# Another map of on-chip memory for one decode step with its gradients: V of seven groups resident, K in two slots

## The chip, the cores and the metric

The kernel runs on one core of a Trainium2 chip. The time is the device time of one execution in microseconds (us); less is better. The core has TensorE (PE in the profile) for matrix products, VectorE (DVE), ScalarE (ACT), GpSimd (POOL) and SyncE (SP), and 16 DMA engines that move data between DRAM and on-chip memory. Two queues feed those DMA engines here: q1, filled by SP, and q0, filled by POOL.

## The reference

One token `x` of 448 numbers goes through a layer norm, attention over a cache (16 query heads, 8 groups of keys and values, head size 256, the last 4096 of 32768 positions), a residual sum, a second layer norm and a gated feed-forward layer without a nonlinearity. Cut to what matters:

```
q = (layernorm(x) @ wq), 16 heads of 256
scores = q . k[:, :, Sk-W:, :] / 16 ;  p = softmax(scores) ;  o = p . v[:, :, Sk-W:, :]
h = x + o @ wo
y = h + ((n @ w_gate) * (n @ w_up)) @ w_down,   n = layernorm(h)
outputs: y, and the gradients of x, k_cache, v_cache, wq, wo, w_gate, w_up, w_down for a given grad_out
```

All data is bf16. The outputs `out_2` and `out_3` are the gradients of the two caches (called dK and dV here) in the caches' full shape, 134 MB each: zero outside the window of 4096 positions, computed inside it. So 235 MB of the outputs are zeros that must be written to DRAM all the same.

## The kernel before

The zeros go out on SP's queue (`FILL`). One memset on VectorE makes a tile `zeros`; then 18 transfers (`fill`, line 63) copy it into the gradients of the caches, 16 KB to a packet, at most eight in flight at a time. A rest of one region is cut over different sets of partitions, which spreads it unevenly over the DMA engines, and two pieces of it (`fill_rest`) go on POOL's queue. Everything else that moves, loads and computed outputs, is issued by POOL (`IO`), in the order in which POOL's program stands; an issue waits there until its source is written or its destination is free, and those behind it wait too.

On chip, the large data lives in nine slots of 16 KB per partition (`S`), an array `Mt` and a ring `Rt`. A slot holds K or V of one group: 128 partitions, 32 positions each, 256 numbers per position. The tables say which group uses which slot:

```
K_SLOT = [6, 7, 8, 6, 7, 8, 6, 7]
V_SLOT = [0, 1, 2, 3, 4, 5, 8, 8]
```

The work has three parts.

The first part runs over the eight groups. `scores` transposes K through TensorE in eight steps of four positions (`products`, line 294: a bank of transposes, an evacuation by ScalarE or VectorE in turn, products with q). `softmax` follows, and then `moments` (lines 346 to 361): in 16 steps of two positions VectorE scales K by the probabilities, and TensorE sums products of V with the scaled K and with the probabilities. The loop issues `softmax(g)`, `scores(g + 1)`, `moments(g)`, with K loaded two groups ahead and V one ahead. V of groups 6 and 7 both pass through slot 8, in halves (`load_V_halves`).

The turn comes next: the output projection with `wo`, the second layer norm, the gate and up products, and the way back through them to the gradient of the attention output and of q. `wo`, `w_gate` and `w_up` are loaded into K slots and into the ring when the last moments are done with them. `spread` makes rows out of columns and copies them to all partitions.

The second part again runs over the groups. It transposes V (line 607) and multiplies it with the gradient of the output (line 612), forms 32 products of rows (line 636), two positions to a PSUM tile of two banks, and evacuates dV and dK apart, ScalarE the one and VectorE the other (line 239 and 241, the helper `evac`). dV is staged in the slot of this group's V, dK in slot 6 or 7, and both are issued to DRAM (line 641). V of groups 6 and 7, which no longer stand on chip, are loaded again after groups 1 and 2 (`load_V`, line 643). Between the groups stand the outer products that make the gradients of the weights (`side`, `outer`, lines 516 and 517), through two staging buffers, and the parts that need `wq` and `w_down` a second time (`dxn_load`, `dxn_part`, `ffn_out`).

Of the kernel before, what the change touches and what calls it, by code (L numbers as in the profile page):

```python
# [13 lines left out]
D = 448  # L14
NI = 7
# [11 lines left out]
NS = 9  # L27
NV = 6
# [6 lines left out]
K_SLOT = [6, 7, 8, 6, 7, 8, 6, 7]  # L35
V_SLOT = [0, 1, 2, 3, 4, 5, 8, 8]
# [3 lines left out]
def kernel(  # L40
# [8 lines left out]
    small = ctx.enter_context(tc.tile_pool(name="small", bufs=2))  # L49
    ps = ctx.enter_context(tc.tile_pool(name="ps", bufs=1, space=bass.MemoryType.PSUM))  # L50

    x_bf = const.tile([1, D], bf16, tag="rowa", name="x_bf")
    FILL.dma_start(out=x_bf[:], in_=A_x.rearrange("a b d -> (a b) d"))
    go_bf = const.tile([1, D], bf16, tag="rowb", name="go_bf")
    FILL.dma_start(out=go_bf[:], in_=grad_out.rearrange("a b d -> (a b) d"))
# [25 lines left out]
    S = const.tile([128, NS, SLOT], bf16)  # L81
    Mt = const.tile([128, G, 2, 2 * Dh], bf16)
    Rt = const.tile([128, SLOT], bf16)

    def slot(k):
        return S[:, k, :]

    def slot_kv(k):
        return S[:, k, :].rearrange("p (t d) -> p t d", d=Dh)

# [12 lines left out]
    def load_V_halves(g):  # L103
        for h in range(2):
            t = slice(h * T // 2, (h + 1) * T // 2)
            IO.dma_start(out=Vw[g][:, t, :], in_=A_v_cache[0, g, Sk - W:, :].rearrange("(p t) d -> p t d", t=T)[:, t, :])
# [5 lines left out]
    wq_sb = S[:, 4:6, :].rearrange("p a b -> p (a b)")[:, 0:NI * HQ]  # L112
# [4 lines left out]
    wd0 = S[:, 3, 0:FC * D].rearrange("p (c n) -> p c n", n=D)  # L117
    wd_rows = B_w_down.rearrange("(s j m) n -> j s (m n)", s=2, j=128)
    IO.dma_start(out=wd0.rearrange("p (s m) n -> p s (m n)", s=2), in_=wd_rows)

# [5 lines left out]
    ones_bf = const.tile([128, 128], bf16)  # L126
# [46 lines left out]
    def rows_to_half(row, xe):  # L173
        t = ps.tile([128, NI], f32, tag="tmp", bufs=1)
        for i in range(NI):
            c = xe[i // 4][:, (i % 4) * 128:(i % 4 + 1) * 128]
            V_.tensor_copy(out=c.rearrange("o (m r) -> o m r", r=2), in_=half_cols(row, i))
            P_.matmul(t[:, i:i + 1], lhsT=c, rhs=ones_f[0:1, 0:1], start=True, stop=True)
        return t
# [64 lines left out]
    xe0 = [Mt[0:1, G - 2 + k].rearrange("p f c -> p (f c)").bitcast(f32) for k in range(2)]  # L244
    xX = const.tile([128, NI], f32)
    V_.tensor_copy(out=xX[:], in_=rows_to_half(x_bf[:], xe0)[:])
    gX = const.tile([128, NI], f32)
    V_.tensor_copy(out=gX[:], in_=rows_to_half(go_bf[:], xe0)[:])
# [17 lines left out]
    q_rows = const.tile([H, Dh], bf16)  # L266
    do_rows = const.tile([H, Dh], bf16)


# [7 lines left out]

    def kt_buf():
        k = kt_ctr[0] % NB
        kt_ctr[0] += 1  # L280
        return Rt[:, k * 1024:(k + 1) * 1024].rearrange("p (i h c) -> p i h c", i=4, h=2)

    def pk_buf():
        k = NB + pk_ctr[0] % NB
        pk_ctr[0] += 1
        return Rt[:, k * 1024:(k + 1) * 1024].rearrange("p (i h d) -> p i h d", i=2, h=2)

    def products(Xw, vecT, g, out_ps):

        for q in range(8):  # L290
            tr = ps.tile([128, 4, 2, 128], bf16, tag="tr", bufs=2)
            for i in range(4):
                for dh in range(2):
                    P_.transpose(tr[:, i, dh, :], Xw[:, 4 * q + i, dh * 128:(dh + 1) * 128], ident_bf[:])  # L294
            xt = kt_buf()
            evac(xt, tr[:])
            for i in range(4):
                for dh in range(2):
                    P_.matmul(out_ps[:, 4 * q + i, :], lhsT=xt[:, i, dh, :], rhs=vecT[:, 4 * g + dh:4 * g + dh + 3:2],
                              start=(dh == 0), stop=(dh == 1))  # L300
# [6 lines left out]
    def scores(g):  # L307
        sT[g] = fps.tile([128, T, 2], f32, tag="sT", bufs=2, name="sT")
        products(Kw[g], qT, g, sT[g])

    def softmax(g):
# [19 lines left out]
        pf = small.tile([128, T, 2], f32, tag="p_f")  # L331
# [344 lines left out]
```

## Time and profile before

| | |
|---|---|
| median of 3 runs | 800.72 us (800.29 to 801.64) |
| the profiled execution: its time, and its span | 800.97 us, 799.2 us |
| bytes moved by the DMA engines | 336.46 MB, mean 421 GB/s |
| read from and written to DRAM | 55.18 MB, 280.59 MB |
| PE, PEld, DVE, ACT, POOL busy | 466.5, 269.7, 378.0, 170.0, 37.6 us |
| first part's last K and V issue by POOL | 251.00 us |
| first and last dV or dK issue | 473.31 and 700.14 us |

The page cuts the span into 40 slices of 20 us: a digit is the busy share in tenths, `DMA` the mean of the 16 engines, `GB/s` what they moved. Its part 3 gives each queue's packets, bytes and the time of those packets as a share of 16 engines' span. A window's line gives start and end, length, busy time of PE, PEld, DVE, ACT and POOL with their instructions in brackets, the granted clock of TensorE, the DMA share and GB/s. A timeline's line gives the start, the duration, engine, line and instruction, and in square brackets how long the engine was idle before and what ended that. An issue's line gives its count, the size of one, and the median us from issue to landing.

### The profile page before, as it was taken

The numbers are of one execution on the slowest core, as the hardware profiler recorded it, in microseconds if no ns is written. First come the engines' busy times: TensorE is split into PE (matmuls) and PEld (weight loads), VectorE is DVE, ScalarE is ACT, GpSimd is POOL, SyncE is SP. The second block draws the span as 40 slices with busy tenths as digits, with TensorE's granted clock in tenths as the row PEclk, the third lists the DMA queues.
The fourth block names the chain that finished last, engine by engine and source line by source line (L and its number), as shares of the span: only waits on it lengthen the run. The fifth ranks groups of instructions, "written<-read, shape, count | busy, mean of one in ns | idle before, by whom it ended". The sixth has DMA issues, their size and how long they took to land.

```text
span 799.2 us, 10787 instructions
## 1 busy us (share of the span) xinstructions
PE 466.5 (58%) x4384; PEld 269.7 (34%) x4419; DVE 378.0 (47%) x1150; ACT 170.0 (21%) x261; POOL 37.6 (5%) x78
## 2 busy tenths in 40 slices
PE   3659767999997644532788645489963625500000
PEld 3545535655664322332576212135510101100000
DVE  5129554778866411668423568375463623500000
ACT  0220202211220000300432322245532413300000
POOL 3000000000000010000001000001000000000000
PEclk9999696999998875555556555555555555555555
DMA  8999999999999999999999999999999999999996
GB/s 340 430 425 430 427 430 430 429 425 429 428 424 421 429 423 429 430 424 431 428 425 423 411 427 432 421 431 420 428 429 426 429 429 417 427 425 429 428 430 294
DMA packets 23815, 336.46 MB, mean 421 GB/s; under 512 B 1501, under 2 KB 1503, under 8 KB 3559
## 3 DMA queue, kind: packets, MB, share of 16 engines
q1 hardware_dynamic: 14550, 231.98, 68.4%
q0 software_dynamic: 9216, 103.80, 30.9%
q8 instruction: 34, 0.56, 0.2%
q14 instruction: 15, 0.12, 0.0%
HBM read 55.18 MB, written 280.59 MB: 420 GB/s over the span
## 4 chain that ended last, share of the span: by engine, by line
DMA 17%; issue 16%; PE 11%; DVE 8%; ACT 3%; POOL 1%; POOLq 0%; ACTq 0%; DVEq 0%
DMA out_dram<-S 7%; DMA Rt<-in_A_wq_dram 4%; DMA S<-in_A_wo_dram 3%; DMA S<-in_A_v_cache_dram 3%; ACT S L239 3%; PE tr L607 3%; PE d_ps L636 2%; DVE S L473 2%; DVE S L241 2%; PE dp L612 1%; PE MT L350 1%; DVE Rt L461 1%; DVE Rt L552 1%; PE dh_ps L188 1%; PE ao L421 1%
## 5 line engine op out<-in xcount | busy, mean ns | idle before, releaser
L636 PE MATMUL d_ps<-R,S 32*128 32x512 bf16 x256 | 121.8, 611 | 88.9 <-DVE S L241 87.7
L350 PE MATMUL MT<-Rt,S 128*128 128x512 bf16 x477 | 137.4, 393 | 7.7 <-DMA S<-in_A_v_cache_dram 7.2
L346 DVE TENSOR_SCALAR Rt<-S,pf 128x256 bf16<-128x256 bf16 x512 | 117.3, 282 | 20.3 <-PE MT L350 12.1
L241 DVE CAST S<-d_ps 128x512 bf16<-128x512 f32 x128 | 86.4, 688 | 54.0 <-ACT S L239 38.8
L239 ACT CAST S<-d_ps 128x512 bf16<-128x512 f32 x128 | 75.0, 586 | 149.3 <-PE d_ps L636 149.1
L636 PEld LDWEIGHTS <-S 32*128 32x128 bf16 x256 | 26.0, 116 | 155.5 <-issue 153.8
L607 PE MATMUL tr<-ident_bf,S 128*128 128x128 bf16 x512 | 66.3, 305 | 17.8 <-ACT S L239 17.8
L294 PE MATMUL tr<-ident_bf,S 128*128 128x128 bf16 x512 | 51.7, 260 | 38.8 <-DMA S<-in_A_k_cache_dram 36.6
L353 PEld LDWEIGHTS <-S 128*128 128x128 bf16 x512 | 47.5, 98 | 57.8 <-issue 3.9
L607 PEld LDWEIGHTS <-S 128*128 128x128 bf16 x512 | 48.5, 137 | 31.9 <-issue 31.9
L294 PEld LDWEIGHTS <-S 128*128 128x128 bf16 x512 | 40.3, 118 | 40.1 <-DMA S<-in_A_k_cache_dram 37.1
L353 PE MATMUL acc<-pT_all,S 128*128 128x2 bf16 x512 | 47.3, 165 | 4.9 <-DMA S<-in_A_v_cache_dram 2.8
L239 ACT COPY Rt<-tr 128x1024 bf16<-128x1024 bf16 x32 | 32.4, 1012 | 71.8 <-PE tr L294 71.4
L356 PE MATMUL acc<-pT_all,S 128*128 128x2 bf16 x512 | 46.9, 164 | 0.0
L239 ACT COPY S<-tr 128x1024 bf16<-128x1024 bf16 x32 | 32.4, 1013 | 49.2 <-PE tr L607 32.2
L241 DVE COPY Rt<-tr 128x1024 bf16<-128x1024 bf16 x32 | 22.0, 688 | 39.5 <-PE tr L294 35.2
L350 PEld LDWEIGHTS <-S 128*128 128x128 bf16 x512 | 35.1, 99 | 15.7 <-DMA S<-in_A_v_cache_dram 7.2
L241 DVE COPY S<-tr 128x1024 bf16<-128x1024 bf16 x32 | 22.0, 688 | 37.1 <-PE tr L607 37.0
L358 ACT CAST Mt<-MT 128x512 bf16<-128x512 f32 x8 | 4.7, 586 | 149.0 <-PE MT L350 132.9
L356 PEld LDWEIGHTS <-S 128*128 128x128 bf16 x512 | 30.8, 97 | 0.2
L612 PEld LDWEIGHTS <-S 128*128 128x128 bf16 x512 | 20.7, 108 | 23.2 <-ACT S L239 16.9
L612 PE MATMUL dp<-doT,S 128*128 128x2 bf16 x512 | 23.7, 169 | 6.1 <-ACT S L239 5.2
(200 smaller groups left out, 394.9 us busy)
## 6 DMA issues: line engine op xcount, KB each, us to landing
out_dram<-zeros SPq DMA_DIRECT2D x15, 14336.0 KB, 164.8
out_dram<-S POOLq DMA_DIRECT2D x16, 2048.0 KB, 29.4
S<-in_A_k_cache_dram POOLq DMA_DIRECT2D x8, 2048.0 KB, 28.4
S<-in_A_v_cache_dram POOLq DMA_DIRECT2D x8, 2048.0 KB, 60.1
out_dram<-zeros SPq DMA_DIRECT2D x1, 10240.0 KB, 95.2
S<-in_A_v_cache_dram POOLq DMA_DIRECT2D x4, 1024.0 KB, 14.2
S<-in_A_wq_dram POOLq DMA_DIRECT2D x1, 3584.0 KB, 15.2
S<-in_A_wo_dram POOLq DMA_DIRECT2D x2, 1792.0 KB, 20.7
```

The costliest lines, as they stand in the source:

```text
L188: P_.matmul(d3[:, :, (7 * s + i) // 2], lhsT=lt, rhs=ident_f[:, s::2], start=(first and n == 0), stop=(n == 2 * NI - 1), skip_group_check= ...
L239: S_.copy(out=out, in_=in_)
L241: V_.tensor_copy(out=out, in_=in_)
L294: P_.transpose(tr[:, i, dh, :], Xw[:, 4 * q + i, dh * 128:(dh + 1) * 128], ident_bf[:])
L346: V_.tensor_scalar(out=pk[:, i, h, :], in0=K[:, t, :], scalar1=pf[:, t, h:h + 1], scalar2=None, op0=ALU.mult)
L350: P_.matmul(MT[:, hf, :], lhsT=Vv[:, t, hf * 128:(hf + 1) * 128], rhs=pk[:, i, :, :].rearrange("p h d -> p (h d)"), start=(t == 0), stop=( ...
L353: P_.matmul(acc[:, 2 * hf:2 * hf + 2], lhsT=Vv[:, t, hf * 128:(hf + 1) * 128], rhs=pT_all[:, g, t, :], start=(t == 0 and hf == 0), stop=(t ...
L356: P_.matmul(acc[:, 4 + dk:7 + dk:2], lhsT=K[:, t, dk * 128:(dk + 1) * 128], rhs=pT_all[:, g, t, :], start=False, stop=(t == T - 1), skip_g ...
L473: V_.tensor_tensor_reduce(out=wo_b(b), in0=wo_b(b), in1=dh_bc[:], scale=1.0, scalar=0.0, op0=ALU.mult, op1=ALU.add, accum_out=doW[:, b:b + 1])
L607: P_.transpose(tr[:, i, dh, :], Vw[g][:, 4 * q + i, dh * 128:(dh + 1) * 128], ident_bf[:])
L612: P_.matmul(dp[:, 4 * q + i, :], lhsT=xt[:, i, dh, :], rhs=doT[:, 4 * g + dh:4 * g + dh + 3:2], start=(dh == 0), stop=(dh == 1))
L636: P_.matmul(d_ps[:, i, :, :].rearrange("p w d -> p (w d)"), lhsT=rows[32 * k:32 * k + 32, a, :], rhs=R[32 * k:32 * k + 32, :], start=True, ...
```

## The change

On-chip memory becomes one array `BIG`: nine slots and a tail. V of groups 0 to 6 has slots 0 to 6 from first load to last use; slots 7 and 8 are for K, each loaded in two halves (`load_halves`) after the moments of the group two before, and V of group 7 takes slot 7 after the moments of group 6 and is the one V that is loaded a second time, into slot 2. The ring of six buffers lies at the end of the tail, `w_gate` and `w_up` behind `wo` in slot 8 and the tail.

In the first part, `moments(g)` issues the eight steps of `scores(g + 1)` after its own steps 4 to 11, each with `issue_after` behind the last matmul of its step, and `softmax(g + 1)` with step 11. `wo` comes in four transfers. At the turn, `spread` keeps its result in PSUM, where the reductions of the weights read it, and is done for one weight after the other. In the second part one position has one PSUM bank with dV and dK, which one engine evacuates, four banks in turn; dV and dK are staged side by side in slots 7 and 8 for even groups and 0 and 1 for odd ones. The outer products have one spare buffer and the slots that come free, and are spread over the groups in another way; their issues and the second loads of `w_down` and `wq` stand behind the dV and dK of their group. Small rows move into the tail, and some small tiles have one buffer where they had two.

```diff
-NS = 9
-NV = 6
...
-K_SLOT = [6, 7, 8, 6, 7, 8, 6, 7]
-V_SLOT = [0, 1, 2, 3, 4, 5, 8, 8]
+KS = 7
+TAIL = 9 * SLOT
+SIZE = TAIL + 10624
+K_SLOT = [KS + g % 2 for g in range(G)]
+V_SLOT = [0, 1, 2, 3, 4, 5, 6, KS]
...
+    BIG = const.tile([128, SIZE], bf16)
+    x_bf = BIG[0:1, TAIL + 2048:TAIL + 2048 + D]
+    FILL.dma_start(out=x_bf, in_=A_x.rearrange("a b d -> (a b) d"))
+    go_bf = BIG[0:1, TAIL + 3072:TAIL + 3072 + D]
+    FILL.dma_start(out=go_bf, in_=grad_out.rearrange("a b d -> (a b) d"))
...
-    def load_V_halves(g):
+    def load_halves(dst, cache, g):
         for h in range(2):
             t = slice(h * T // 2, (h + 1) * T // 2)
-            IO.dma_start(out=Vw[g][:, t, :], in_=A_v_cache[0, g, Sk - W:, :].rearrange("(p t) d -> p t d", t=T)[:, t, :])
+            IO.dma_start(out=dst[:, t, :], in_=cache[0, g, Sk - W:, :].rearrange("(p t) d -> p t d", t=T)[:, t, :])
...
-    wq_sb = S[:, 4:6, :].rearrange("p a b -> p (a b)")[:, 0:NI * HQ]
+    wq_sb = BIG[:, 4 * SLOT:4 * SLOT + NI * HQ]
     IO.dma_start(out=wq_sb, in_=flat_rows(A_wq))
     load_K(0)
     load_V(0)
     load_K(1)
-    wd0 = S[:, 3, 0:FC * D].rearrange("p (c n) -> p c n", n=D)
+    load_V(1)
+    wd0 = slot(6)[:, 0:FC * D].rearrange("p (c n) -> p c n", n=D)
     wd_rows = B_w_down.rearrange("(s j m) n -> j s (m n)", s=2, j=128)
     IO.dma_start(out=wd0.rearrange("p (s m) n -> p s (m n)", s=2), in_=wd_rows)
+    load_V(2)
...
+    def products(Xw, vecT, g, out_ps, q):
+        tr = ps.tile([128, 4, 2, 128], bf16, tag="tr", bufs=2)
+        for i in range(4):
+            for dh in range(2):
+                P_.transpose(tr[:, i, dh, :], Xw[:, 4 * q + i, dh * 128:(dh + 1) * 128], ident_bf[:])
...
+    def scores(g, q):
+        if q == 0:
+            sT[g] = fps.tile([128, T, 2], f32, tag="sT", bufs=2, name="sT")
+        products(Kw[g], qT, g, sT[g], q)
...
-                    P_.matmul(acc[:, 4 + dk:7 + dk:2], lhsT=K[:, t, dk * 128:(dk + 1) * 128], rhs=pT_all[:, g, t, :],
+                    mm = P_.matmul(acc[:, 4 + dk:7 + dk:2], lhsT=K[:, t, dk * 128:(dk + 1) * 128], rhs=pT_all[:, g, t, :],
                               start=False, stop=(t == T - 1), skip_group_check=True)
+            if g + 1 < G and 4 <= c < 12:
+                with tc.issue_after(mm.ins):
+                    scores(g + 1, c - 4)
+                if c == 11:
+                    softmax(g + 1)
...
-    woA = S[:, 6, 0:16 * D].rearrange("p (b n) -> p b n", n=D)
-    woB = S[:, 8, 0:16 * D].rearrange("p (b n) -> p b n", n=D)
-    wg_sb = S[:, 7, 0:NI * HF]
-    wu_sb = Rt[:, 0:NI * HF]
-    bc2 = [S[:, 7, NI * HF:NI * HF + F].rearrange("p (i c) -> p i c", i=2), Rt[:, NI * HF:NI * HF + F].rearrange("p (i c) -> p i c", i=2)]
+    A0 = KS * SLOT
+    WB = [0, 9, 18, 27, 32]
 
     def wo_b(b):
-        return woA[:, b, :] if b < 16 else woB[:, b - 16, :]
-
-    scores(0)
-    rows16(qT, q_rows[:], SCALE)
+        o = A0 + b * D if b < 18 else A0 + SLOT + (b - 18) * D
+        return BIG[:, o:o + D]
+
+    def load_wo(k):
+        o = A0 + (k // 2) * SLOT + (k % 2) * 9 * D
+        n = WB[k + 1] - WB[k]
+        IO.dma_start(out=BIG[:, o:o + n * D].rearrange("p (b n) -> p b n", n=D), in_=wo_v[:, WB[k]:WB[k + 1], :])
+
+    G0 = A0 + SLOT + 14 * D
+    wg_sb = BIG[:, G0:G0 + NI * HF]
+    wu_sb = BIG[:, G0 + NI * HF:G0 + 2 * NI * HF]
+    bc2 = [BIG[:, TAIL + w * F:TAIL + (w + 1) * F].rearrange("p (i c) -> p i c", i=2) for w in range(2)]
+
+    for q in range(8):
+        scores(0, q)
+    softmax(0)
     for g in range(G):
-        if g + 1 < NV:
-            load_V(g + 1)
+        if g + 3 < G - 1:
+            load_V(g + 3)
+        moments(g)
         if g + 2 < G:
-            load_K(g + 2)
-        if g >= NV:
-            load_V_halves(g)
-        if g == G - 1:
-            IO.dma_start(out=woA, in_=wo_v[:, 0:16, :])
-        softmax(g)
-        if g + 1 < G:
-            scores(g + 1)
-        moments(g)
+            load_halves(Kw[g + 2], A_k_cache, g + 2)
+        if g + 2 == G:
+            load_halves(Vw[G - 1], A_v_cache, G - 1)
...
-    IO.dma_start(out=woB, in_=wo_v[:, 16:32, :])
+    for k in (0, 2, 1, 3):
+        load_wo(k)
...
-    def spread(dst, src, nb, rows2, row_blocks):
-
-        for b0 in range(0, nb, 4):
-            n = min(4, nb - b0)
-            t = fps.tile([2, 4, 128], f32, tag="sT", bufs=2, name="t")
+    def spread(src, nb, b0):
+
+        bc = tps.tile([128, 2, 1024], f32, tag="bc", name="bc")
+        for b1 in range(b0, min(b0 + 8, nb), 4):
+            n = min(4, nb - b1)
+            t = tps.tile([2, 4, 128], f32, tag="t", name="t")
             for j in range(n):
-                P_.matmul(t[:, j, :], lhsT=src[:, b0 + j:b0 + j + nb + 1:nb], rhs=ident_bf[:], start=True, stop=True)
-            evac(row_blocks[:, b0:b0 + n, :], t[:, 0:n, :])
-        for i2 in range(2):
-            for b0 in range(0, nb, 4):
-                n = min(4, nb - b0) * 128
-                t = fps.tile([128, 512], f32, tag="sT", bufs=2, name="t")
-                P_.matmul(t[:, 0:n], lhsT=Par[:, i2, :], rhs=rows2[:, b0 * 128:b0 * 128 + n], start=True, stop=True)
-                evac(dst[:, i2, b0 * 128:b0 * 128 + n], t[:, 0:n])
-
-    rows2 = [S[0:2, k, 16 * D:16 * D + HF] for k in (6, 8)]
-    for w in range(2):
-        spread(bc2[w], dgu[:, w, :], NI, rows2[w], rows2[w].rearrange("s (j m) -> s m j", m=NI))
+                P_.matmul(t[:, j, :], lhsT=src[:, b1 + j:b1 + j + nb + 1:nb], rhs=ident_bf[:], start=True, stop=True)
+            r = small.tile([2, 4, 128], bf16, tag="R", name="r")
+            evac(r[:, 0:n, :], t[:, 0:n, :])
+            for i2 in range(2):
+                P_.matmul(bc[:, i2, (b1 - b0) * 128:(b1 - b0 + n) * 128], lhsT=Par[:, i2, :], rhs=r[:, 0:n, :].rearrange("p b c -> p (b c)"),
+                          start=True, stop=True)
+        return bc
...
+        bc = spread(dgu[:, w, :], NI, 0)
+        wv = w_sb.rearrange("p (i j m) -> p i m j", i=NI, m=NI)
         for i in range(NI):
-            V_.tensor_tensor_reduce(out=wv[:, i, :], in0=wv[:, i, :], in1=bc2[w][:, i % 2, :], scale=1.0, scalar=0.0,
+            V_.tensor_tensor_reduce(out=wv[:, i], in0=wv[:, i], in1=bc[:, i % 2, 0:HF].rearrange("p (m j) -> p m j", m=NI), scale=1.0, scalar=0.0,
                                     op0=ALU.mult, op1=ALU.add, accum_out=P2[:, w, i:i + 1])
+        for i2 in range(2):
+            S_.copy(out=bc2[w][:, i2, :].rearrange("p (j m) -> p m j", m=NI), in_=bc[:, i2, 0:HF].rearrange("p (m j) -> p m j", m=NI))
...
+    wd1 = slot(3)[:, 0:FC * D].rearrange("p (c n) -> p c n", n=D)
+
+    def wd_load():
+        IO.dma_start(out=wd1.rearrange("p (s m) n -> p s (m n)", s=2), in_=wd_rows)
...
+    PAIR = [KS, 0, KS, 0, KS, 0, KS, 0]
     side = {
-        0: [o67_job(0, 0, 4), o67_job(0, 4, 7), lambda: dxn_part(0, 4), lambda: dxn_load(4, 7)],
-        1: [lambda: dxn_part(4, 7), dx_out],
-        2: [o5_job(0), o5_job(8)],
-        3: [o5_job(16), o5_job(24)],
-        4: [lambda b=b: outer(o8[b // 7], b, b + 7, lambda n: dh2_bc[:], hh, D) for b in (0, 7)],
-        5: [o4_job(0), o4_job(2)],
-        6: [o4_job(4), o4_job(6)],
+        0: [o67_job(spare, 1, 4, 7)],
+        1: [o67_job(spare, 0, 0, 4)],
+        2: [o67_job(spare, 0, 4, 7), lambda: load_V(G - 1)],
+        3: [o5_job(spare, 0), wd_load],
+        4: [lambda: dxn_load(0, 4), ffn_out, o5_job(spare, 8), o5_job(half(3, 0), 16), o5_job(half(3, 1), 24)],
+        5: [lambda: dxn_load(4, 7), lambda: dxn_part(0, 4), o8_job(spare, 0), o8_job(half(4, 0), 7), o4_job(half(4, 1), 0)],
+        6: [lambda: dxn_part(4, 7), dx_out, o4_job(half(5, 0), 2), o4_job(half(5, 1), 4), o4_job(spare, 6)],
         7: [],
     }
-    ffn_out()
-    o67_job(1, 0, 4)()
-    o67_job(1, 4, 7)()
-    dxn_load(0, 4)
+    o67_job(spare, 1, 0, 4)()
...
-        R = small.tile([128, 2 * Dh], bf16, tag="R")
-        S_.copy(out=R[:], in_=R_ps[:])
-        stg = [Vw[g], slot_kv(6 + g % 2)]
-        for c in range(T // 2):
-            d_ps = bps.tile([128, 2, 2, Dh], f32, tag="d2", bufs=2)
-            for i in range(2):
-                t = 2 * c + i
-                k, a = t // 8, t % 8
-                P_.matmul(d_ps[:, i, :, :].rearrange("p w d -> p (w d)"), lhsT=rows[32 * k:32 * k + 32, a, :], rhs=R[32 * k:32 * k + 32, :],
-                          start=True, stop=True)
-            for w in range(2):
-                evac(stg[w][:, 2 * c:2 * c + 2, :], d_ps[:, :, w, :])
+            P_.matmul(R_ps[:, k * Dh:(k + 1) * Dh], lhsT=ex[:].rearrange("h a r -> h (a r)"), rhs=rr, start=True, stop=True)
+        R = Rb[:, g % 2, :]
+        S_.copy(out=R, in_=R_ps[:])
+        pair = BIG[:, PAIR[g] * SLOT:(PAIR[g] + 2) * SLOT].rearrange("p (w t d) -> p w t d", w=2, d=Dh)
+        for t in range(T):
+            d_ps = bps.tile([128, 2, Dh], f32, tag="d2", bufs=4)
+            k, a = t // 8, t % 8
+            P_.matmul(d_ps[:].rearrange("p w d -> p (w d)"), lhsT=rows[32 * k:32 * k + 32, a, :], rhs=R[32 * k:32 * k + 32, :],
+                      start=True, stop=True)
+            evac(pair[:, :, t, :], d_ps[:])
         for w, o in ((0, out_3), (1, out_2)):
-            IO.dma_start(out=o[0, g, Sk - W:, :].rearrange("(p t) d -> p t d", t=T), in_=stg[w])
-        if 1 <= g <= G - NV:
-            load_V(NV + g - 1)
...
```

## The prediction

> **What bounds the kernel now.** I read four views in this order. First the page's slices and its part on the queues, to see whether an engine or the transfers fill the span:
>
> ```profile
> PEclk9999696999998875555556555555555555555555
> DMA  8999999999999999999999999999999999999996
> GB/s 340 430 425 430 427 430 430 429 425 429 428 424 421 429 423 429 430 424 431 428 425 423 411 427 432 421 431 420 428 429 426 429 429 417 427 425 429 428 430 294
> ...
> q1 hardware_dynamic: 14550, 231.98, 68.4%
> q0 software_dynamic: 9216, 103.80, 30.9%
> ...
> HBM read 55.18 MB, written 280.59 MB: 420 GB/s over the span
> ```
>
> Between the first slice and the last the 16 DMA engines are full, at 411 to 432 GB/s, whatever TensorE's granted clock does. The two queues' packets took 68.4 + 30.9 = 99.3% of the 16 engines' span. The bound is the sum of all transfers; what is left to ask is whether anything lies behind them. So, second, a table of windows, with the end in stretches of its own:
>
> ```profile
> 216.00:252.00 36.00, 34.31 (x437) 21.96 (x442) 25.93 (x107) 5.87 (x10) 2.65 (x5) 0.95 1.00 424
> 500.00:700.00 200.00, 127.45 (x638) 46.42 (x636) 96.79 (x174) 73.88 (x118) 12.22 (x23) 0.50 1.01 426
> 700.00:739.00 39.00, 0.00 (x0) 0.00 (x0) 0.00 (x0) 0.00 (x0) 0.53 (x1) 0.50 1.01 425
> 739.00:782.00 43.00, 0.00 (x0) 0.00 (x0) 0.00 (x0) 0.00 (x0) 0.00 (x0) 0.50 1.01 428
> 782.00:799.20 17.20, 0.00 (x0) 0.00 (x0) 0.00 (x0) 0.00 (x0) 0.00 (x0) 0.50 0.64 274
> ```
>
> After 700 us no compute engine does anything. Third, the timeline of POOL and SP and the issues by size:
>
> ```profile
> 491.76 0.61 POOL L95 DMA_DIRECT2D S<-in_A_v_cache_dram  x1 [17.19 <-DMA out_dram<-S]
> ...
> 531.24 0.55 POOL L95 DMA_DIRECT2D S<-in_A_v_cache_dram  x1 [23.84 <-DMA out_dram<-S]
> ...
> 700.14 0.53 POOL L641 DMA_DIRECT2D out_dram<-S  x1 [0.19 <-issue]
> ```
> ```profile
> out_dram<-S POOLq DMA_DIRECT2D x16, 2048.0 KB, 29.4
> S<-in_A_k_cache_dram POOLq DMA_DIRECT2D x8, 2048.0 KB, 28.4
> ...
> S<-in_A_v_cache_dram POOLq DMA_DIRECT2D x4, 1024.0 KB, 14.2
> ```
>
> POOL's queue carries everything that is computed; it issues its last output at 700.14, and by the packet records the last packet of q0 ends at 737.4. From there to the end only SP's zero fill runs. That is the cover of this kernel: computed output could land some 56 us later (to about 794, the mean end of the 16 engines) before it, and not the sum of the bytes, sets the end. The two rows at 491.76 and 531.24 are V of groups 6 and 7, read a second time.
>
> **The change part by part.** Durations are of the profiled execution (span 799.2, its own time 800.97, which is 0.25 above the median of 800.72). A packet's duration is from the trace's packet records: 16 KB takes 617 ns on average (611 at best), 8 KB 314, 14 KB 535, a semaphore write 9. Work on one engine is one sixteenth of the sum, since a transfer over 128 partitions gives each engine 8 packets.
>
> 1. V of group 6 is not read again: 128 packets x 617 ns / 16 = -4.94 us. The window 739 to 782 says the same: 2.097 MB at 428 GB/s is 4.90 us. Group 7 is still read twice.
>
> 2. K of groups 2 to 7 comes in halves, packets of 8 KB for 16 KB: 6 x (256 x 314 - 128 x 617) / 16 = +0.53 us. Bounds: 0, since 216 to 252, where the four V halves run, holds 424 GB/s with the engines at 1.00; and +1.2, by the 95th percentile of an 8 KB packet, 321 ns. I take the mean. V of group 6, in halves before, now comes whole at its first read: -0.09.
>
> 3. A_wo in four transfers (packets of 8064, 8064, 8064 and 4480 bytes) for two of 14 KB: 128 x (3 x 309 + 175 - 2 x 535) / 16 = +0.26, with 309 and 175 estimated from the 8 KB, 6 KB (240) and 4 KB (159) packets. Bounds 0 and +0.4.
>
> 4. POOL issues 69 transfers of data for 63. Six more semaphore writes per engine of 9 ns are +0.05; the six issues of 0.53 us lie on POOL, beside a full fill queue.
>
> The Trainium skill, "DMA: Bandwidth & Descriptors", section "Anatomy of one DMA — SWDGE (gpsimd) path", speaks against halves: every transfer costs a fixed 2.0 us besides its bytes. Six more would be an estimated 12 us, and the sum 808.5. The trace disagrees where it can be seen: through 216 to 252 halves run at the rate of the whole. That cost falls on the waiting reader there, not on the engines.
>
> 5. The scores of the next group go into the moments' loop, between the matmuls of its pairs 4 to 11, and K has two slots for three. The instructions are the same, so only waits change. TensorE runs in order: behind a transpose that waits for a half of K stand the rest of the moments' matmuls, and behind those VectorE's scaled K tiles. A group of moments and scores takes 24.4 us now (K issues at 152.26, 176.62, 200.97). The second half can be issued only when the moments end, lands 14.2 us later, and is wanted at pair 8 of 16, about 12 us in: 2 us of stall, six times, is 12 us. Bounds: 0, and 6 x 28.4 = 170 us if a whole load were exposed each time. I take 12, nearest to the 14.2 row. It lies wholly under the 56 us.
>
> 6. dV and dK of one token now share a PSUM bank that one engine evacuates, four banks deep. Now two pairs of tokens take 2.41 us, of which TensorE works 1.86 (626.02, 628.43, 630.83 in the chain; VectorE waits 38.8 us for ScalarE over the run): 19.3 us a group. Then TensorE bounds it at 8 x 1.86 = 14.9, since 16 evacuations of 688 ns are 11.0. Between 0 and -4.4 us a group, I take -3, so -24 over eight. The staging pair of two groups earlier must have landed; a pair is issued some 50 us before (two groups' evacuations and products) and lands in 29.4.
>
> 7. Around the turn: the spreads go one weight at a time through PSUM, the row copies have two buffers, A_wo arrives in smaller packets beside 16 KB fill packets. About +15 us at most, from the 282 to 388 stretch (106 us). In the second half the outer products move behind the dV and dK transfers on POOL, so the first of these is issued sooner than at 473. V 1 and V 2 are issued ahead of the identity matrices: 2 x 0.53 us, under the wait for K (36.6 us in all before those transposes). SP's queue keeps its 18 fills in order, behind the same memset of 3.47 us.
>
> Steps 5 to 7 come to 12 - 24 + 15 = +3 us on the last output, worth nothing: 56 us of fill cover it. Sum: -4.94 + 0.53 - 0.09 + 0.26 + 0.05 = -4.19. The profiled execution would take 796.8, the median 796.5.
>
> **The rivals.**
>
> A. The forecast. Its own range: 16 KB packets lost 7.7 us per engine against 611 ns, in bursts (0.87 us of it in 440 to 460); a change of the mix may move that by a quarter, 2 us either way. 794.6 to 798.4.
>
> B. The saving is eaten, within 0.2%. The 8 KB packets at 321 ns and A_wo at its bound leave -4.94 + 1.2 + 0.4 = -3.3, and more bursts would have to give back another 2 us: 799.1 to 802. The even 424 to 429 GB/s over such different mixes speaks against it.
>
> C. Computed output becomes the last to land. Place: TensorE waiting for a half of K inside the moments, six groups. Price: at 28.4 us each the last output is issued at 870; with the fill drained its 4.2 MB take 10 us, so about 882. It decides from the point where the last issue slips from 700 to about 782, which is 82 / 6 = 13.7 us of stall a group, seven times what I took. For it: every computed transfer stands in one queue. Against it: step 6 gives time back.
>
> D. Each added transfer leaves the engines idle between issue and first packet. The row: A_wq, alone at the start, is issued at 1.30 and its first packet starts at 2.91, so 1.6 us; six times is 9.6: 806. For it: the start, with one queue filled, has 339 GB/s in 20 us. Against it: from 20 us on the fill always has packets waiting. This is the mechanism that the 2.0 us of the Trainium skill's page would need.
>
> E. The second read is not gone, or another took its place: 801. The order of issues in the changed kernel has nine V transfers' worth for ten, so only a slip in what I read could make it so; under 1 in 100, counted with B.
>
> **How the numbers follow.** A has 0.86, B 0.06, C 0.05, D 0.03. No change means within 0.2% of 800.72, 799.1 to 802.3, about what this kernel's runs can tell (they spread over 1.35 us). So faster 0.86, same 0.06, slower 0.08. The predicted time is A's, 796.5. The range is A's widened a little to the unknown costs, 794.6 to 798.8; it leaves out the other cases.
>
> **What would show it.** HBM read 53.08 MB for 55.18 (step 1), written 280.59 as before. In the second half one load of V for two. The slices at 420 to 432 GB/s also where K comes in halves (steps 2, 3, and D). A last output issued between 660 and 760, and a stretch of at least 30 us at the end with the compute engines empty (steps 5 to 7); if that stretch is missing, C is true. VectorE's wait for ScalarE on the PSUM tiles nearly gone (step 6). The prediction would be wrong if 16 KB packets took more than 620 ns on average, or if the last stretch, where the engines end between 782 and 798, grew: an engine that ends alone costs its whole lag.

## The result, and the profile after

The changed kernel takes 811.70 us (median of 4 runs, 811.53 to 812.44), the kernel before 801.08 (median of its 4 runs beside them). The ratio is 1.0135, 95% interval 1.0118 to 1.0153: slower by 1.35%, where 796.5 was forecast. The profiled execution took 811.53, its span is 809.8.

The page of the changed kernel, its DMA slices, queues and traffic:

```profile
DMA  8999999999999999999999999999999999999954
GB/s 342 429 426 427 434 431 426 429 427 427 425 426 428 424 425 424 431 429 431 433 431 428 427 426 426 425 425 425 425 424 420 417 427 431 415 427 426 379 235 207
...
q1 hardware_dynamic: 14550, 231.98, 67.4%
q0 software_dynamic: 10080, 101.70, 30.1%
...
HBM read 53.09 MB, written 280.59 MB: 412 GB/s over the span
```

The transfers did what was forecast: 2.1 MB are read less, and the packets' time is 792.2 us per engine against 795.9 before (summed over the packet records, divided by 16), -3.7 for the forecast's -4.19. 16 KB packets take 617.6 ns in both. But the span is longer than that sum by 17.6 us, against 3.3 before, and what is lost lies in the last three slices. The table of windows of the changed kernel over its end (start and end, length, PE, PEld, DVE, ACT, POOL, clock, DMA share, GB/s):

```profile
700.00:740.00 40.00, 13.98 (x36) 4.13 (x35) 26.44 (x44) 9.79 (x18) 5.49 (x6) 0.50 1.01 422
740.00:760.00 20.00, 5.73 (x15) 1.47 (x12) 5.53 (x8) 4.00 (x7) 1.05 (x2) 0.50 0.99 396
760.00:780.00 20.00, 4.90 (x35) 3.83 (x36) 12.21 (x20) 0.59 (x1) 2.11 (x4) 0.59 0.76 320
780.00:800.00 20.00, 12.56 (x32) 3.40 (x29) 11.07 (x16) 9.11 (x16) 1.05 (x2) 0.50 0.45 184
800.00:810.00 10.00, 0.00 (x0) 0.00 (x0) 0.00 (x0) 0.00 (x0) 0.00 (x0) 0.50 0.56 236
```

Before, compute was empty from 700 on and the engines were full to 782. Now compute runs until 794 and the engines run dry: the fill's last packet ends at 761.5 (797.7 before), q0's at 805.8 (737.2 before). The roles of the two queues have changed over. The timeline of POOL in the changed kernel shows when the outputs were issued, and two rows of its first part that matter below:

```profile
32.44 1.09 POOL L98 DMA_DIRECT2D BIG<-in_A_v_cache_dram  x2 [23.55 <-PE q_ps L261]
56.93 0.53 POOL L109 DMA_DIRECT2D BIG<-in_A_k_cache_dram  x1 [23.39 <-DVE BIG L349]
...
490.94 1.07 POOL L658 DMA_DIRECT2D out_dram<-BIG  x2 [44.80 <-DVE BIG L247]
559.41 0.53 POOL L533 DMA_DIRECT2D out_dram<-Mt  x1 [67.41 <-DVE Mt L532]
559.94 1.05 POOL L658 DMA_DIRECT2D out_dram<-BIG  x2
...
794.63 1.05 POOL L658 DMA_DIRECT2D out_dram<-BIG  x2 [15.91 <-issue]
```

The last pair of dV and dK is issued at 794.63 for 700.14, so 94.5 us later. The forecast had +3. Three places in the trace account for lateness.

First, the turn. Groups of the changed kernel by line (count, then busy us and mean ns, then idle time before):

```profile
L475 DVE CUSTOM_DVE_ANT_0 BIG<-BIG,bc 128x896 bf16<-128x896 bf16 x14 | 48.8, 3764 | 1.8 <-PE bc L466 1.8
L478 ACT CAST BIG<-bc 128x896 bf16<-128x896 f32 x4 | 14.2, 3770 | 25.9 <-DVE P L475 25.9
```

The same fourteen in the kernel before:

```profile
L461 DVE CUSTOM_DVE_ANT_0 S<-S 128x896 bf16<-128x896 bf16 x7 | 7.6, 1109 | 0.1
L461 DVE CUSTOM_DVE_ANT_0 Rt<-Rt 128x896 bf16<-128x896 bf16 x7 | 7.2, 1088 | 0.0
```

The change reads and writes the weights in the order "p i m j", a step of 7 elements or 14 bytes, and each now takes 3.76 us. The gradient of q (`dq`) is written at 444.5, 378.8 before: 66 us, of which 16.5 were already there at the end of the first part (last `kbar` 301.0 for 284.5).

Second, the first part. TensorE's waits in the changed kernel (us in total, times, the longest):

```profile
PE tr L296 <- DMA BIG<-in_A_k_cache_dram: 67.2, 6, 50.4
```

One wait of 50.4 us, from 71.4 to 121.8: the first half of K of group 2, issued at 56.93. By then 12.0 MB of q0 had landed, `wq`, K and V of groups 0 and 1; still ahead of it in the queue were a weight of 1.6 MB and V of groups 2 to 5 (the last two are the row at 32.44), 10.0 MB in all. Beside the fill q0 moved 0.18 MB per us (21.6 MB at 110), so they took 55 us. The other five waits together are 16.8 us.

Third, the second part. POOL waits 67.4 us before its issue at 559.41 (line 533, the outer product placed behind group 0). VectorE in the changed kernel, just before:

```profile
556.39 0.69 DVE L247 COPY BIG<-tr 128x1024 bf16<-128x1024 bf16 x1 [1.93 <-PE tr L627]
557.55 0.23 DVE L637 TENSOR_TENSOR df<-dp,delta 128x64 f32<-128x64 f32 x1 [0.47 <-PE dp L632]
...
557.95 1.54 DVE L532 TENSOR_SCALAR Mt<-BIG,xf 128x896 bf16<-128x896 bf16 x4
```

The four multiplications that make this outer product stand in VectorE's program behind the evacuations of V's transposes for later groups (`tr`, `dp`), which come early. The multiplications wait there, POOL waits for them, and dV and dK of group 1, evacuated at 517, wait behind POOL until 559.94.

### The profile page after: what moved, and what is told of

It reads as the page before. It is cut to its first block, busy times and chain, and to the rows that moved or that the text cites. A ratio compares the mean times of both kernels' runs of the same rounds, so it can differ in the third digit from the quotient of the medians.

```text
span 809.8 us, 10847 instructions
## 1 busy us (share of the span) xinstructions
PE 451.0 (56%) x4419; PEld 258.3 (32%) x4419; DVE 408.8 (50%) x1144; ACT 175.6 (22%) x259; POOL 42.8 (5%) x84
## 3 DMA queue, kind: packets, MB, share of 16 engines
q1 hardware_dynamic: 14550, 231.98, 67.4%
## 4 chain that ended last, share of the span: by engine, by line
PE 38%; DMA 25%; DVE 15%; another core or an unknown queue 12%; ACT 4%; issue 2%; POOL 0%; POOLq 0%; ACTq 0%; DVEq 0%
DMA BIG<-in_A_k_cache_dram 10%; PE MT L353 9%; PE d_ps L654 8%; DMA BIG<-in_A_v_cache_dram 6%; DVE BIG L475 6%; PE tr L627 5%; DMA out_dram<-Mt 5%; DMA BIG<-in_A_wo_dram 4%; PE tr L296 3%; ACT BIG L245 3%; DVE BIG L489 2%; PE dp L632 2%; DVE BIG L571 2%; PE sT L301 1%
## 5 line engine op out<-in xcount | busy, mean ns | idle before, releaser
L349 DVE TENSOR_SCALAR BIG<-BIG,pf 128x256 bf16<-128x256 bf16 x512 | 111.2, 281 | 76.8 <-PE MT L353 75.1
L353 PE MATMUL MT<-BIG 128*128 128x512 bf16 x512 | 140.4, 393 | 4.7 <-DMA BIG<-in_A_v_cache_dram 4.7
L654 PE MATMUL d_ps<-BIG 32*128 32x512 bf16 x256 | 109.3, 600 | 47.8 <-ACT BIG L245 24.8
L245 ACT COPY BIG<-tr 128x1024 bf16<-128x1024 bf16 x64 | 64.8, 1012 | 246.2 <-PE tr L296 179.6
L247 DVE CAST BIG<-d_ps 128x512 bf16<-128x512 f32 x128 | 87.0, 690 | 59.1 <-PE d_ps L654 38.0
L245 ACT CAST BIG<-d_ps 128x512 bf16<-128x512 f32 x128 | 72.9, 588 | 89.6 <-PE d_ps L654 69.7
L296 PE MATMUL tr<-ident_bf,BIG 128*128 128x128 bf16 x512 | 47.8, 237 | 67.4 <-DMA BIG<-in_A_k_cache_dram 67.2
L627 PE MATMUL tr<-ident_bf,BIG 128*128 128x128 bf16 x512 | 63.3, 286 | 27.1 <-ACT BIG L245 23.3
L654 PEld LDWEIGHTS <-BIG 32*128 32x128 bf16 x256 | 27.3, 119 | 107.6 <-issue 95.3
L627 PEld LDWEIGHTS <-BIG 128*128 128x128 bf16 x512 | 44.3, 127 | 44.7 <-issue 40.8
L296 PEld LDWEIGHTS <-BIG 128*128 128x128 bf16 x512 | 33.6, 105 | 69.0 <-DMA BIG<-in_A_k_cache_dram 67.7
L353 PEld LDWEIGHTS <-BIG 128*128 128x128 bf16 x512 | 41.2, 100 | 29.4 <-DMA BIG<-in_A_v_cache_dram 5.2
L356 PEld LDWEIGHTS <-BIG 128*128 128x128 bf16 x512 | 39.4, 100 | 32.9 <-issue 5.9
L475 DVE CUSTOM_DVE_ANT_0 BIG<-BIG,bc 128x896 bf16<-128x896 bf16 x14 | 48.8, 3764 | 1.8 <-PE bc L466 1.8
L356 PE MATMUL acc<-pT_all,BIG 128*128 128x2 bf16 x512 | 41.0, 165 | 2.9 <-DVE kbar L369 1.4
L359 PE MATMUL acc<-pT_all,BIG 128*128 128x2 bf16 x512 | 40.4, 164 | 0.0
L359 PEld LDWEIGHTS <-BIG 128*128 128x128 bf16 x512 | 29.3, 97 | 0.1
L632 PEld LDWEIGHTS <-BIG 128*128 128x128 bf16 x512 | 20.5, 106 | 24.8 <-ACT BIG L245 11.6
```

The lines of the kernel that those rows point to most:

```text
L245: S_.copy(out=out, in_=in_)
L247: V_.tensor_copy(out=out, in_=in_)
L349: V_.tensor_scalar(out=pk[:, i, h, :], in0=K[:, t, :], scalar1=pf[:, t, h:h + 1], scalar2=None, op0=ALU.mult)
L353: P_.matmul(MT[:, hf, :], lhsT=Vv[:, t, hf * 128:(hf + 1) * 128], rhs=pk[:, i, :, :].rearrange("p h d -> p (h d)"), start=(t == 0), stop=( ...
L356: P_.matmul(acc[:, 2 * hf:2 * hf + 2], lhsT=Vv[:, t, hf * 128:(hf + 1) * 128], rhs=pT_all[:, g, t, :], start=(t == 0 and hf == 0), stop=(t ...
L359: mm = P_.matmul(acc[:, 4 + dk:7 + dk:2], lhsT=K[:, t, dk * 128:(dk + 1) * 128], rhs=pT_all[:, g, t, :], start=False, stop=(t == T - 1), s ...
```

## The experiments

Theory S: the time is the later of two ends, the byte sum of all transfers and the landing of POOL's queue; the cover of 56 us was there, and three lots of lateness added up to more than it. Rival P: the order on VectorE in the second part alone set the end, the rest stayed covered. Rival Q: lateness ahead of 564 us costs nothing. Each of the first three kernels mends one place in the changed kernel, and the fourth all of them.

**The turn without the step of 7.** The row is made in PSUM in two halves of 448, in the weights' own order, so that reductions and copies run over neighbours:

```diff
+            if nb == NI:
+                for i2 in range(2):
+                    for h in range(2):
+                        P_.matmul(bc[:, i2, 512 * h:512 * h + 448].rearrange("p (j m) -> p m j", m=NI)[:, b1:b1 + n, :], lhsT=Par[:, i2, :],
+                                  rhs=r[:, 0:n, 64 * h:64 * h + 64], start=True, stop=True)
+                continue
-        wv = w_sb.rearrange("p (i j m) -> p i m j", i=NI, m=NI)
+        wv = w_sb.rearrange("p (i h c) -> p i h c", i=NI, h=2)
```

> The changed kernel with the reductions of the gate and up weights reading rows in their stored order (the PSUM row is written in two halves, so that weight and row are walked without a stride), nothing else changed. Theory S (the time is now set by when POOL's last output lands, and lateness adds up from several places): the 14 reductions go from 3.76 to about 1.0 us and the four copies from 3.77 to about 1.0, so the first of these outputs leaves about 43 us sooner, POOL's last output lands near 763 instead of 806, the fill ends last again, and the time is 796.5 to 799. Rival P (the order of VectorE's work in the second part alone sets the end, what comes before it is swallowed): the reductions are as fast, the last output lands after 795, and the time stays at 808 to 812.

Measured: 798.82 us, ratio to the kernel before 0.9969 (0.9958 to 0.9980). Its groups at the turn:

```profile
L482 DVE CUSTOM_DVE_ANT_1 BIG<-BIG,bc 128x896 bf16<-128x896 bf16 x14 | 14.3, 1084 | 3.0 <-PE bc L468 3.0
L485 ACT CAST BIG<-bc 128x896 bf16<-128x896 f32 x4 | 3.4, 909 | 6.1 <-DVE P L482 6.1
```

With the same operand in PSUM the reductions take 1084 ns: the step is what costs, not PSUM. 14 x (3.764 - 1.084) = 37.5 us, and the first dV and dK are issued 37.0 us sooner, at 453.92. The last come at 767.33, 27.3 sooner. Lateness ahead of 450 us cost 12.9 us of time, so Q falls, and P with it, since the order in the second part is untouched. Two points of the expectation were missed: q0's last packet lands at 793.5 and not near 763, and the fill does not end last: its last packet is at 780.1.

**K ahead of V in POOL's queue.** V of groups 3 to 6 is issued behind the K halves of the same group of the loop:

```diff
-        if g + 3 < G - 1:
-            load_V(g + 3)
...
-            load_halves(Kw[g + 2], A_k_cache, g + 2)
+            k_load = load_halves(Kw[g + 2], A_k_cache, g + 2)
+        if g + 3 < G - 1:
+            with tc.issue_after(k_load.ins):
+                load_V(g + 3)
```

> The changed kernel with V of groups 3 to 6 issued behind both halves of K of the group one before, so that K of group 2 no longer stands behind V of groups 3, 4 and 5 in POOL's queue. Theory S: TensorE's wait for K of group 2 falls from 50 to 10 to 25 us, the first part ends 10 to 17 us sooner, POOL's last output lands as much sooner, and the time is 797 to 803. Rival P: the wait falls as much, but the time stays at 808 to 812.

Measured: 801.59 us, ratio 1.0013 (0.9991 to 1.0036); ten runs spread from 798.55 to 806.46, where the other kernels spread by 0.5 to 2.2 us; why was not followed. TensorE's waits for K in this kernel:

```profile
PE tr L297 <- DMA BIG<-in_A_k_cache_dram: 39.3, 7, 18.1
```

The long wait is 18.1 us for 50.4. The last `kbar` comes at 278.7, 22.3 us sooner than in the changed kernel (10 to 17 were expected) and 5.8 sooner than before the change. The first dV is issued at 468.99, 22.0 sooner, the last at 783.94, 10.7 sooner. The profiled execution took 800.84, 16.9 us after that issue; in the changed kernel it is 811.53 - 794.63 = 16.9 as well. So here POOL's queue still sets the end in full.

**The order in the second part.** VectorE's work for group g is queued behind the multiplications of the outer products that follow group g - 2 (`ends` holds the last of them for each group; the body of the loop over groups stands inside):

```diff
+        with ExitStack() as order:
+            if g >= 2:
+                order.enter_context(tc.issue_after(ends[g - 2].ins))
...
+        ends.append(job_end[0])
```

> The changed kernel with VectorE's work on group g+2 of the second part queued behind the outer product that follows group g, so that POOL, which stands at that outer product's transfer, is not held while VectorE prepares four more groups. Theory S: the 46 us in which POOL's queue is empty after the first group (518 to 564) shrink to under 10, the last output lands 25 to 40 us sooner, time 797 to 800. Rival P agrees on this run. Rival Q (from 564 on POOL's queue is never empty, so only its total matters, and holes before that cost nothing): the hole goes, the time stays within 2 us of 811.7.

Measured: 798.43 us, ratio 0.9966 (0.9953 to 0.9978). POOL in this kernel:

```profile
488.87 1.07 POOL L662 DMA_DIRECT2D out_dram<-BIG  x2 [44.79 <-DVE BIG L247]
510.77 0.53 POOL L534 DMA_DIRECT2D out_dram<-Mt  x1 [20.83 <-DVE Mt L533]
511.29 1.05 POOL L662 DMA_DIRECT2D out_dram<-BIG  x2
...
757.43 1.06 POOL L662 DMA_DIRECT2D out_dram<-BIG  x2 [17.51 <-issue]
```

The wait of 67.4 us is 20.8, and the second pair leaves 22 us behind the first, where it was 69. The last issue is 37.2 us sooner. Its landing is only 13.2 us sooner (792.6 for 805.8; 25 to 40 were expected), since it comes 35 us after the issue, for 11 in the changed kernel: here the fill still runs beside it, until 785.9. The mechanism of the third place is shown; but the first kernel gained as much without it.

**All three.**

> The three edits together. Theory S: the last computed output lands between 690 and 745, the fill ends last, and the time is the one that was forecast from the bytes, 796 to 798, below the kernel before by about 4 us. If halves of K and more transfers cost the engines time of their own (the forecast's rival D), it stays at 801 or above although the last output lands early.

Measured: 796.23 us, ratio 0.9941 (0.9926 to 0.9956), faster than both kernels. First dV at 432.85, last at 700.23: the three places took back 94.4 of the 94.5 us. Alone they took back 27.3 + 10.7 + 37.2 = 75.2; what the singly mended kernels lose again lies, in the kernel with the turn mended, late in the second part (its last two pairs of dV and dK are 56.1 us apart, 47.4 in the changed kernel), and was not followed further. That the last issue falls on the 700.14 of the kernel before is chance: the first dV leaves 40.5 us sooner than there, and from the first issue to the last it takes 267.4 us for 226.8. Windows of its end:

```profile
700.00:740.00 40.00, 0.00 (x0) 0.00 (x0) 0.00 (x0) 0.00 (x0) 1.05 (x2) 0.50 1.01 427
740.00:760.00 20.00, 0.00 (x0) 0.00 (x0) 0.00 (x0) 0.00 (x0) 0.00 (x0) 0.50 1.01 431
760.00:780.00 20.00, 0.00 (x0) 0.00 (x0) 0.00 (x0) 0.00 (x0) 0.00 (x0) 0.50 0.99 421
```

This is the end of the kernel before again, with its cover: the fill's last packet at 793.7, q0's at 752.1, which is 7 us past the range of the expectation.

**One read less in the kernel before.** The second read of V of group 6 is left out, nothing else; that group's part of dK is then worked out from what lies in the slot:

```diff
-        if 1 <= g <= G - NV:
+        if g == 2:
             load_V(NV + g - 1)
```

> The kernel before without the second read of V of group 6 (that group's part of the key gradient and of the query's side is then worked out from what lies in the slot, so this part of the computation is left out). It measures step 1 of the forecast by itself: 2.1 MB less on full engines. Theory S and the forecast: 4.9 us less, 796 to 796.5; last output of POOL's queue issued at 690 to 702. If the saved bytes are not worth their share of the engines (the forecast's rival B), 799 or more.

Measured: 795.96 us, ratio 0.9940 (0.9925 to 0.9955), -5.1 us for the forecast's -4.94. The kernel with all three mends has in addition the halves of K, A_wo in four and six more transfers, and takes 0.27 us longer, less than either spreads (0.5 and 1.0); the packets' time is 791.2 us per engine in both. Steps 2 to 4 came to +0.75 in the forecast.

**The step of 7 in the kernel before.** Its reductions take the changed kernel's order of elements, all operands in SBUF:

```diff
-        wv = w_sb.rearrange("p (i c) -> p i c", i=NI)
+        wv = w_sb.rearrange("p (i j m) -> p i m j", i=NI, m=NI)
```

> The kernel before with the 14 reductions of the gate and up weights walking weight and row with a stride of seven elements, as the changed kernel does, and nothing else. Both theories expect 3.5 to 3.9 us per reduction for 1.1 if the stride is what costs (1.1 to 1.3 if it was the operand in PSUM). Theory S: the last output is issued 30 to 38 us later, at 730 to 738, under the cover of the fill, and the time stays within 0.2% of the kernel before. If lateness always costs, the time rises by 30 us or a good part of it.

Measured: 800.99 us, ratio 0.9999 (0.9990 to 1.0008). Its two groups:

```profile
L461 DVE CUSTOM_DVE_ANT_1 S<-S 128x896 bf16<-128x896 bf16 x7 | 25.2, 3695 | 0.1
L461 DVE CUSTOM_DVE_ANT_1 Rt<-Rt 128x896 bf16<-128x896 bf16 x7 | 24.6, 3800 | 0.0
```

The last issue comes 36.0 us later, at 736.19, and the time does not move. The same step that costs the changed kernel 12.9 us costs this one nothing.

**More of the same delay.** In front of the reductions, fourteen copies of the weights onto themselves with the same step (which change nothing in the data), and then three passes of them:

```diff
+        for _ in range(3):
+            for i in range(NI):
+                V_.tensor_copy(out=wv[:, i], in_=wv[:, i])
```

> As the last, with 14 copies of the weights onto themselves with the same stride ahead of the reductions: a second dose of delay at the same place, some 25 to 50 us. Theory S: the cover ends where POOL's last issue passes about 775 to 780, as read from the runs of the changed kernel (767 at 798.8, 784 at 801.6, 795 at 811.7); so with a last issue at 760 to 775 the time is 800.5 to 803, with one at 790 it is 807 to 812. If the two doses cost in proportion, the time rises by twice what the single dose cost.

> The kernel before with the strided reductions and three passes of fourteen strided copies of w_sb onto itself ahead of them (one pass moved the last issue by 22 us, from 736.19 to 758.15). No transfer is changed. Theory S (the time is the later of the byte sum and the landing of POOL's queue): three passes move the last issue by 3 x 22 = 66 to 3 x 32 = 96 us, to 802 to 832; that is past the cover's end, so the time rises, to some 17 us behind the last issue (the distance in the changed kernel, 794.6 to 811.7): 819 to 849. The rival Q (lateness ahead of 564 us costs nothing, whatever its size): 801, as with one pass. A third reading, that late outputs cost in proportion from the first microsecond and the two smaller doses were only lost in the noise (0.1 us at 58): 801.5 at most.

One pass: 800.88 us, ratio 1.0001 (0.9991 to 1.0011), last issue 758.15. Three passes: 816.68 us (two runs), ratio 1.0196 (1.0166 to 1.0226). POOL and the windows of the end with three passes:

```profile
800.96 0.53 POOL L644 DMA_DIRECT2D out_dram<-S  x1 [0.19 <-issue]
```
```profile
760.00:780.00 20.00, 12.86 (x29) 2.95 (x29) 11.51 (x17) 7.62 (x13) 0.53 (x1) 0.50 0.68 288
780.00:800.00 20.00, 14.95 (x33) 3.21 (x31) 11.75 (x18) 9.96 (x17) 1.60 (x3) 0.50 0.57 237
```

58.0 us of lateness cost nothing, 100.8 us cost 15.8 (against 800.85 beside it). No transfer differs: the packets' time is 796.4 and 796.5 us per engine, and with three passes the fill's last packet ends at 764.0. The end is 16.0 us behind the last issue (816.95 - 800.96), and issue and time came 1 and 2 us under the ranges of S. So the edge lies near 801 - 16.5 = 784.5, an estimate, since no run of this kernel has its last issue between 758 and 801. Q and a cost in proportion from the first microsecond both fall: at 58 us of 101, a proportional cost would have been 9.

**The two-bank tile again.** The kernel with all three mends, but with two positions to a tile of two banks and dV and dK to different engines, as before the change:

```diff
-            for t in range(T):
-                d_ps = bps.tile([128, 2, Dh], f32, tag="d2", bufs=4)
...
+            for c in range(T // 2):
+                d_ps = bps.tile([128, 2, 2, Dh], f32, tag="d2", bufs=2)
...
+                for w in range(2):
+                    evac(pair[:, w, 2 * c:2 * c + 2, :], d_ps[:, :, w, :])
```

> The three edits together, with the staging of dV and dK back to two positions in two banks, dV evacuated by one engine and dK by the other. It measures step 6 by itself: a group's 32 products take 19.3 us for about 14, the last output is issued 15 to 40 us later than 700. Theory S: no change in time, 796 to 797. If the evacuation by banks had been part of the loss, this would be faster than the three edits.

Measured: 796.98 us, ratio 0.9956 (0.9941 to 0.9970), last issue 714.72. VectorE's wait for ScalarE is back in this kernel:

```profile
DVE BIG L248 <- ACT BIG L246: 56.1, 87, 2.8
```

It was 38.8 us before the change, and the kernel with all three mends has no such row. The bank per engine is worth 14.5 us of the last issue, just under the 15 to 40 expected; under the cover the intervals of the two kernels overlap, and no difference in time is shown.

The runs side by side; "floor" is the time of the same bytes with an early last issue:

| kernel | last issue, us | median, us | floor, us |
|---|---|---|---|
| before | 700.14 | 801.08 | |
| before, step of 7 | 736.19 | 800.99 | 801.1 |
| before, one pass more | 758.15 | 800.88 | 801.1 |
| before, three passes more | 800.96 | 816.68 | 801.1 |
| changed, three mends | 700.23 | 796.23 | |
| the same, two-bank tile | 714.72 | 796.98 | 796.2 |
| changed, order mended | 757.43 | 798.43 | 796.2 |
| changed, turn mended | 767.33 | 798.82 | 796.2 |
| changed, K ahead of V | 783.94 | 801.59 | 796.2 |
| changed | 794.63 | 811.70 | 796.2 |

A maximum of the floor and the last issue plus 16 to 17 us fits all rows but two (the kernel with K ahead of V within its spread): with the order or the turn mended alone the kernel is 2.2 and 2.6 us above its floor, though its last issue is 13 to 23 us ahead of the edge at 796.5 - 16.5 = 780. The kernel before at 758.15 shows nothing of the kind.

The packet records show where these 2 us are. In both kernels q0's last packet is the last of all, at 793.5 (turn) and 792.6 (order), behind the fill's at 780.1 and 785.9. The last transfer ends no later than with all three mends, 793.7. But in all five kernels in which q0 ends last, the profiled execution's time is 5.6 to 5.8 us behind that packet, and in the six in which the fill ends last it is 3.3 us behind the fill's. So the two ends differ by some 2.4 us in what still follows them. What makes up this difference the records don't show.

## Why the prediction was wrong

**Steps 1 to 4 held.** The read left out is worth 5.1 us (4.94 forecast), the halves and the added transfers together a few tenths. Rival B and rival D fall with that, though D's 806 lies close to the measured time. That is chance: the engines are full until 755, the missing time lies after that, and the same transfers in the mended kernel take 796.23. The fixed 2.0 us per transfer of the Trainium skill ("DMA: Bandwidth & Descriptors", section "Anatomy of one DMA — SWDGE (gpsimd) path"), which gave 808.5 when it was counted as time of the engines, is none in these runs.

**The cover held.** The forecast put it at some 56 us; 58 us of delay in the kernel before cost nothing. Counted by the last issue it is wider, some 84 us up to the estimated edge, as the forecast's rival C has it (82).

**What failed is the size of steps 5 to 7:** "12 - 24 + 15 = +3 us on the last output" was +94.5. Of that, 16.5 - 14.5 + 49 + 37 = 88 is placed below; the rest was not traced.

- Step 7 is the main failure. "About +15 us at most" for the turn was 49 (`dq` 66 later, less the 16.5 that came with the first part). 37 of it are the step of 7 elements in the reductions, for which the sum has no term: step 7 names the spreads, the row copies and A_wo, and not the reductions, whose rows of 1109 and 1088 ns were for neighbouring elements. The other 12 are within the 15.
- Step 7 also looked at the outer products only on POOL, and concluded that the first dV would be issued sooner. It did not ask where their multiplications stand on VectorE. They stand behind the evacuations of later groups, and since POOL issues in order, dV and dK of the next group wait as well: 37.2 us of the last issue.
- Step 5's 12 us was 16.5 on the last `kbar`, a fair size by another mechanism. The stalls that it described, for the other five K loads, are 16.8 us together, 3.4 each for the 2 forecast. What it did not see is the load of K of group 2 behind four loads of V: it took 28.4 us, then 14.2, for the time of a load, but this one landed behind the 10.0 MB that were issued ahead of it in its queue. With K issued ahead of V the first part ends 5.8 us sooner than before the change, so the new first part as a whole is a gain.
- Step 6 was right in kind and too large: VectorE's wait for ScalarE is gone, and the gain on the last issue is 14.5 us, measured with the other mends in place, for 24.

**The trace before had the price of the step.** The old `spread` evacuated its rows for the gate and up weights with the same step of 7 in the output (tile `S`), and its row for `dq` without it (tile `Mt`):

```profile
L239 ACT CAST S<-t 2x512 bf16<-2x512 f32 x2 | 4.3, 2137 | 8.3 <-PE t L445 8.3
L241 DVE CAST S<-t 2x384 bf16<-2x384 f32 x2 | 3.3, 1627 | 0.6 <-PE t L445 0.6
L239 ACT CAST Mt<-t 2x512 bf16<-2x512 f32 x2 | 1.2, 576 | 0.9 <-PE t L445 0.9
```

That is 4.2 ns an element on either engine, for 1.1 on ScalarE without the step. For 896 elements it makes 3.7 to 3.8 us, an estimate that the 3764 and 3770 ns of the changed kernel bear out, and fourteen times the difference to 1.1 us would have put some 37 us into step 7.

**Rival C happened, at another place.** Computed output is the last to land, and the sign that the forecast named for it, no empty stretch at the end, is there. Its deciding point, a last issue at about 782, agrees with the edges worked out from the runs (780 and 784.5). Its place, halves of K awaited inside the moments in all six groups, is wrong: but for the one wait of 50.4 us, these waits come to 16.8 us. It had 0.05 because its price was asked of one cause; three causes did it together, 37 and 22 us ahead of the first dV and 36 behind it (from first issue to last 303.7 us, 267.4 with the three mends), and none of them alone covers the 80 us from 700 to the edge. Two readings of packet times in the prediction are 0.2 us late by the profile's own zero: q0 ends at 737.2, and the first packet starts at 2.67, so rival D's 1.6 us is 1.4. Nothing hangs on either.

## What to carry to other kernels

Where slack covers a change, add up the lateness of all its parts against the slack, and give each part a bound that the trace supports: an instruction whose access order changes is priced from a row with that order, on another instruction if need be (here an evacuation of two partitions), and not from its own old row. For every issue in a queue that is moved, follow the producer too: on which engine its work stands, and behind what. For every load, count the bytes ahead of it in its queue, not its own.

## What the runs showed of the hardware

A step of 14 bytes between bf16 elements costs VectorE's multiply-and-reduce over 896 elements a factor of 3.5 (3764 ns for 1084), whether its other operand is in PSUM or, with the same step, in SBUF (3695 and 3800 ns). ScalarE's copy of 896 elements from PSUM, whose output alone has the step in SBUF, goes from 909 to 3770 ns. VectorE's plain copy of 896 elements with the step on both sides takes 2.29 us (one pass in the kernel before). No other step was run.

The Trainium skill, "Advanced Engine Details and Errata", section "SBUF Cachelines", says that an access pays when it falls on another 16-byte line than the one before, with no figure. The runs agree in kind, by these factors. That the line, and not the step as such, sets the price is not shown.
